# A retention block feeding a two-matmul block: writing the first four steps out by hand, scaling the first chunks on VectorE, and moving the transposes

## The chip, the cores and the metric

The kernel runs on one core of a Trainium2 chip. The metric is the device time of one execution in microseconds (us). A profile is one traced execution. Its span (795.6 us for the kernel before) is about 2 us shorter than the execution's time. TensorE does the matmuls; PSUM is the memory in which the kernel has it put its results, in banks of 128 x 512 float32. "Granted clock" is the share of TensorE's full clock that the profile shows; a group of matmuls that runs at about half of it is called cold here, one at full clock warm. "Step" below means one column group of the second block: h = x w_in for 256 tokens and 256 columns, the nonlinearity, and o += g w_out.

## The reference, cut to what matters

```python
# q, k, v: (4, 8, 768, 64) float32; w_in (512, 2048), w_out (2048, 512) float64
for t in range(S):                                   # retention, as a recurrence
    state = gamma * state + k_t outer v_t
    y_t = q_t @ state / sqrt(64)
x = y.transpose(0, 2, 1, 3).reshape(3072, 512)
h = x @ w_in
out = (h - tanh(h)) @ w_out
```

## The kernel before

The recurrence is computed in 24 chunks of 128 tokens. For a chunk, q and v are scaled by powers of gamma (`scale_chunk`), k and q are transposed on TensorE (`turn`) and copied out of PSUM by ScalarE (`turn_copy`), k'v and k q' are formed (`products`, then mask and states on VectorE), and y is accumulated in two halves (`outputs`). Between the halves other matmuls may stand; ScalarE also touches y there (the "seen" copies). The weights come as float64: 32 pieces, each turned into float32 by two ScalarE, four VectorE and two GpSimd instructions (`convert`). Pieces 0 to 3 are columns of w_in, 4 to 7 rows of w_out, and so on. The first h needs pieces 0 and 1, the second 2 and 3, the first o pieces 4 and 5, the second o 6 and 7.

```python
    def scale_chunk(ci):
        ...
            nc.gpsimd.tensor_tensor(t, t, g[...].to_broadcast([P, H, D]), op=ALU.mult)

    def outputs(ci, meanwhile):
        ...
        intra(True)                  # first half of y
        ...                          # the "seen" copies on ScalarE
        meanwhile()                  # a turn or an up stands here
        intra(False)                 # second half
        nc.scalar.copy(out=xT..., in_=y)
        products(ci + 1)             # the next chunk's mask and states

    for ci in range(AHEAD):          # AHEAD = 3: the start
        scale_chunk(ci + 2)
        outputs(ci, lambda: turn(ci + 2, "h"))
        load_chunk(ci + 3)
        turn_copy(ci + 2)
        convert(ci)
        load_weights(ci + 3)
    for s, (n, m2, first, last) in enumerate(steps):     # from here on h (up), shrink, o (downs)
        ...
```

The order is made by hand (`manual_schedule`): each engine gets its instructions in the order of the calls.

Of the kernel before, what the change touches and what calls it, by code (L numbers as in the profile page):

```python
# [11 lines left out]
U32 = mybir.dt.uint32  # L12
# [3 lines left out]
P = 128  # L16
# [15 lines left out]
def kernel(  # L32
# [20 lines left out]
    nc = tc.nc  # L53
    B, H, S, D = q.shape
    NP = H // 2
# [9 lines left out]
    BANK = 512  # L65
# [45 lines left out]
    def weight_ends(i):  # L111


        f, r = divmod(i, 2 * NC)
        if r < NC:
            c, cols = 2 * (r % 2), ds(BANK * f + TH * (r // 2), TH)
            src = w_in[:, cols].rearrange("(c two p) n -> c two p n", two=2, p=D)

            return w1[:, ds(c, 2), cols], [(0, 0, c, 0, src), (1, 0, c, 1, src),
                                           (0, 1, c + 1, 1, src), (1, 1, c + 1, 0, src)]  # L120
        m = NC * f + r - NC
        return w2[:, m], w_out[ts(m, P)]

    def load_weights(i):
        if i >= NW:
            return
        dst, src = weight_ends(i)
        raw = None
        if w_out.dtype != F32:
            raw = stage.tile([P, 2 * BANK], U32, tag="raw", name=f"raw_{i}", bufs=3)  # L130
            raws[i] = raw
        if not isinstance(src, list):
            if raw is None:
                nc.sync.dma_start(out=dst, in_=src)
            else:
                nc.sync.dma_start(out=raw, in_=src.bitcast(U32))
            return
        for half, k, c, which, w in src:
            r = ds(D * half, D)
            if raw is None:  # L140
                nc.sync.dma_start(out=dst[r, k], in_=w[c, which])
            else:
                nc.sync.dma_start(out=raw[r, ts(k, BANK)], in_=w[c, which].bitcast(U32))  # L143

    def convert(i):

# [37 lines left out]
    def load_chunk(ci):  # L184
        if ci >= NCH:
            return
        b, j = divmod(ci, CPB)
        loaded[ci] = []
        for nm, src in (("k", k), ("q", q), ("v", v)):
            t = inp.tile([P, H, D], F32, tag=nm, name=f"{nm}_{ci}")  # L190
            nc.sync.dma_start(out=t, in_=src[b, :, ts(j, P), :].rearrange("h p d -> p h d"))  # L191
            loaded[ci].append(t)

    def scale_chunk(ci):
        if ci >= NCH:
            return
        j = ci % CPB
        _, qh, vh = loaded[ci]
        for t, g in ((qh, gq), (vh, gv)):
            nc.gpsimd.tensor_tensor(  # L200
                t, t, g[:, ts(j, H)][:, :, None].to_broadcast([P, H, D]), op=ALU.mult
            )

# [27 lines left out]
    def products(ci):  # L231

        if ci >= NCH:
            return
        kh, _, vh = loaded[ci]
        kT, qT = (turned[ci][:, i] for i in range(2))
        sp = banks(f"s_{ci}")
        halves = sp.rearrange("p r (w n t) -> p r w n t", w=2, n=NP)
        for p in range(NP):
            for a in range(2):  # L240
                for i in range(2):
                    h, r = 2 * p + i, ds(D * a, D)
                    nc.tensor.matmul(halves[ds(D * i, D), a, 1, p], kh[r, h], vh[r, h],  # L243
                                     start=True, stop=True, skip_group_check=True)
        for p in range(NP):
            for a in range(2):
                for i in range(2):
                    r = ds(D * i, D)
                    nc.tensor.matmul(halves[ds(D * a, D), i, 0, p], kT[r, p, ts(a, D)],  # L249
                                     qT[r, p, ts(a, D)], start=True, stop=True,  # L250
                                     skip_group_check=True)
        m = mid.tile([P, 2, NP, D], F32, tag="a", name=f"a_{ci}")
        nc.vector.tensor_tensor(m, halves[:, :, 0],  # L253
                                causal[:, None, None, :].to_broadcast([P, 2, NP, D]),
                                op=ALU.mult)
        masked[ci] = m
        j = ci % CPB
        if j == 0:
            states[ci] = mid.tile([P, 2, NP, D], F32, tag="state", name=f"state_{ci}", bufs=3)
            nc.vector.tensor_copy(states[ci][:, 1], halves[:, 0, 1])  # L260
        else:
            nc.vector.tensor_tensor(states[ci][:, 1], halves[:, 0, 1], states[ci][:, 0],
                                    op=ALU.add)
        if j < CPB - 1:
            nxt = mid.tile([P, 2, NP, D], F32, tag="state", name=f"state_{ci + 1}", bufs=3)
            nc.vector.tensor_tensor(nxt[:, 0], halves[:, 1, 1], states[ci][:, 1], op=ALU.add)
            states[ci + 1] = nxt

    def outputs(ci, meanwhile):


        j = ci % CPB
        n, nj = divmod(ci, BLK)
        if nj == 0:
            xT[n] = xp.tile([P, NP, BLK * P], F32, tag="xT", name=f"xT_{n}")
        vh = loaded.pop(ci)[2]
        qT = turned.pop(ci)[:, 1]
        a_, st = masked.pop(ci), states.pop(ci)
        yT = banks(f"y_{ci}")
        y = yT[:, :, : 2 * P].rearrange("p r (n t) -> p r n t", n=2)  # L280
        begun = set()

        def to_y(p, i, a, lhsT, rhs):

            col = (i + p) % 2
            start = (p % 2, col) not in begun
            begun.add((p % 2, col))
            nc.tensor.matmul(y[ds(D * col, D), p % 2, p // 2, ts(a, D)], lhsT, rhs,  # L288
                             start=start, stop=True, skip_group_check=True)

        def inter(a):
            for p in range(NP):
                for i in range(2):
                    r = ds(D * i, D)
                    to_y(p, i, a, st[r, a, p], qT[r, p, ts(a, D)])

        def intra(first):
            for pp in range(NP // 2):
                for i in range(2):
                    for a in range(2):  # L300

                        for col in range(2):
                            p = 2 * pp + ((a + col) % 2 if first else (a + col + 1) % 2)
                            if (i + p) % 2 != col:
                                continue
                            r = ds(D * a, D)
                            to_y(p, i, a, vh[r, 2 * p + i], a_[r, i, p])

        if j:
            inter(0)  # L310
        inter(1)
        intra(True)


        flat = yT.rearrange("p r w -> p (r w)")
        for col in range(2):
            r = ds(D * col, D)
            s0, s1 = 2 * P - 1 - D, BANK + 2 * P - 1
            if col:
                s0, s1 = 2 * P - 1, BANK + 2 * P - 1 - D  # L320
            nc.scalar.copy(out=seen[r], in_=flat[r, s0 : s1 + 1 : s1 - s0])
        meanwhile()
        intra(False)
        nc.scalar.copy(  # L324
            out=xT[n][:, :, ts(nj, P)].rearrange("p (n r) t -> p r n t", r=2), in_=y
        )
        products(ci + 1)


    gT = {}  # L330
# [72 lines left out]
    runs += [[(n, m2) for m2 in range(NM // 2)] for n in range(4, 2 * NB)]  # L403
    steps = [(n, m2, i == 0, i == len(r) - 1) for r in runs for i, (n, m2) in enumerate(r)]



    AHEAD = 3
    when = [0, 1, 2, 3, 4] + list(range(5, 28, 2)) + [28, 29, 30, 31]
    with_chunk = {s: AHEAD + i for i, s in enumerate(when)}  # L410
    with_weights = {0: [3, 4], 1: [5, 6], 2: [7]}
    for i in range(8, NW):
        with_weights[i - 5] = [i]

    load_chunk(0)
    load_chunk(1)
    load_weights(0)
    load_weights(1)
    load_chunk(2)
    load_weights(2)  # L420
    scale_chunk(0)
    turn(0)
    turn_copy(0)
    scale_chunk(1)
    products(0)
    turn(1)
    turn_copy(1)
    for ci in range(AHEAD):
        scale_chunk(ci + 2)
        outputs(ci, lambda: turn(ci + 2, "h"))  # L430
        load_chunk(ci + 3)
        turn_copy(ci + 2)
        convert(ci)
        load_weights(ci + 3)
    waiting = []

    def downs(lag):
# [2 lines left out]
            for j in range(2):  # L440
                down(n, m2, j, first, last)

    for s, (n, m2, first, last) in enumerate(steps):
        for i in with_weights.get(s, []):
            convert(i)
            load_weights(i + 3)
        ci = with_chunk.get(s)
        if ci is None:
            up(n, m2)
        else:  # L450
            scale_chunk(ci + 2)
            outputs(ci, lambda: up(n, m2))
            load_chunk(ci + 3)
        shrink(n, m2)
        waiting.append((n, m2, first, last))
        downs(LAG)
        if ci is not None:
            turn(ci + 2)
            turn_copy(ci + 2)
# [57 lines left out]
```

## Time and profile before

| | before |
|---|---|
| median of the runs | 798.71 us at first (3), 798.47 with one run more |
| span of the profiled run | 795.6 us |
| TensorE busy | 760.5 us, 96% |
| TensorE idle up to 90 us, from stretches of 5 us | 31.0 us |
| lost to the lower clock up to 90 us (busy time x (1 - granted clock), the same stretches) | 13.9 us |

The last two rows are the whole room, the 4.7 us of the first load included: after 80.5 us TensorE is full at full clock until the tail. The lines that show it stand in the prediction.

### The profile page before, as it was taken

The numbers are of one execution on the slowest core, as the hardware profiler recorded it, in microseconds if no ns is written. First come the engines' busy times: TensorE is split into PE (matmuls) and PEld (weight loads), VectorE is DVE, ScalarE is ACT, GpSimd is POOL, SyncE is SP. The second block draws the span as 40 slices with busy tenths as digits, with TensorE's granted clock in tenths as the row PEclk, the third lists the DMA queues.
The fourth block names the chain that finished last, engine by engine and source line by source line (L and its number), as shares of the span: only waits on it lengthen the run. The fifth ranks groups of instructions, "written<-read, shape, count | busy, mean of one in ns | idle before, by whom it ended". The sixth has DMA issues, their size and how long they took to land.

```text
span 795.6 us, 13784 instructions
## 1 busy us (share of the span) xinstructions
PE 760.5 (96%) x5504; PEld 515.9 (65%) x5504; DVE 508.4 (64%) x798; ACT 368.2 (46%) x660; POOL 131.0 (16%) x116
## 2 busy tenths in 40 slices
PE   4558999999999999999999999999999999999997
PEld 3446776666676677666666666666666666666663
DVE  0377777778888876566565666565565666655654
ACT  1344666556565644444444444444444444444442
POOL 2355344335433451000000000000000000000000
PEclk8577999999999999999999999999999999999999
DMA  9555564335444413000000000000000000000000
GB/s 201 140 135 130 121 134 110 105 94 132 111 105 99 116 41 81 29 27 27 1 26 1 0 27 0 1 26 1 1 27 1 15 12 0 28 0 1 27 0 26
DMA packets 85967, 42.97 MB, mean 54 GB/s; under 512 B 76560, under 2 KB 76688, under 8 KB 85904
## 3 DMA queue, kind: packets, MB, share of 16 engines
q1 hardware_dynamic: 85760, 41.95, 21.2%
q8 instruction: 43, 0.70, 0.4%
q10 hardware_dynamic: 144, 0.15, 0.1%
q14 instruction: 20, 0.16, 0.1%
HBM read 35.80 MB, written 6.29 MB: 53 GB/s over the span
## 4 chain that ended last, share of the span: by engine, by line
PE 91%; DVE 3%; POOL 2%; SPq 1%; issue 1%; DMA 1%; ACT 1%; DVEq 0%; POOLq 0%; ACTq 0%
PE h L342 41%; PE o L374 41%; PE y L288 3%; PE kqTp L215 3%; PE s L249 1%; PE s L243 1%; POOL low L171 1%; SPq L191 1%; SPq L143 1%; DMA q<-in_q_dram 1%; POOL w L175 1%; POOL q L200 1%; DVE head L168 1%; DVE head L166 0%; DVE power L170 0%
## 5 line engine op out<-in xcount | busy, mean ns | idle before, releaser
L342 PE MATMUL h<-xT,w 128*128 128x256 f32 x1536 | 351.9, 382 | 0.0
L374 PE MATMUL o<-w,g 128*128 128x512 f32 x768 | 347.2, 595 | 0.5 <-DVE g L366 0.5
L342 PEld LDWEIGHTS h<-xT,w 128*128 128x128 f32 x1536 | 291.1, 191 | 67.5 <-issue 30.4
L374 PEld LDWEIGHTS o<-w,g 128*128 128x128 f32 x768 | 144.2, 190 | 144.8 <-issue 136.8
L351 ACT ACTIVATE u<-h 128x512 f32<-128x512 f32 x96 | 57.4, 598 | 265.0 <-PE h L342 265.0
L356 DVE TENSOR_TENSOR th<-h,th 128x512 f32<-128x512 f32 x96 | 66.2, 690 | 158.2 <-ACT th L352 158.2
L366 DVE COPY_PREDICATED g<-large,th 128x512 f32<-128x512 int32 x96 | 71.6, 745 | 9.9
L359 DVE SCALAR_TENSOR_TENSOR h<-q,h 128x512 f32<-128x512 f32 x96 | 66.9, 696 | 10.0
L361 DVE SCALAR_TENSOR_TENSOR h<-q,h 128x512 f32<-128x512 f32 x96 | 66.8, 696 | 10.0
L353 ACT ACTIVATE q<-u,tab 128x512 f32<-128x512 f32 x96 | 69.5, 724 | 0.0
L354 ACT ACTIVATE q<-u,tab 128x512 f32<-128x512 f32 x96 | 69.1, 720 | 0.0
L355 ACT ACTIVATE large<-u,tab 128x512 f32<-128x512 f32 x96 | 68.8, 717 | 0.0
L365 DVE TENSOR_TENSOR g<-h,u 128x512 f32<-128x512 f32 x96 | 66.3, 691 | 3.3
L253 DVE TENSOR_TENSOR a<-s,tab 128x512 f32<-128x512 f32 x24 | 16.6, 692 | 77.5 <-PE s L249 77.5
L171 POOL TENSOR_TENSOR low<-low,power 128x512 f32<-128x512 f32 x32 | 40.9, 1279 | 152.9 <-DVE power L170 151.7
L357 DVE SCALAR_TENSOR_TENSOR h<-u,h 128x512 f32<-128x512 f32 x96 | 65.8, 685 | 0.0
L352 ACT ACTIVATE th<-h 128x512 f32<-128x512 f32 x96 | 57.1, 595 | 0.0
L324 ACT COPY xT<-y 128x512 f32<-128x512 f32 x24 | 14.1, 586 | 92.7 <-PE y L288 92.7
L225 ACT COPY kqT<-kqTp 128x1024 f32<-128x1024 f32 (+1 forms) x27 | 24.5, 920 | 41.6 <-PE kqTp L215 41.6
L175 POOL TENSOR_TENSOR w<-low,head 128x512 f32<-128x512 f32 x32 | 41.0, 1282 | 2.5
L215 PE MATMUL kqTp<-tab,q 128*128 128x128 f32 x96 | 17.3, 310 | 17.0 <-POOL q L200 17.0
L200 POOL TENSOR_TENSOR q<-q,tab 128x512 f32<-128x512 f32 x24 | 25.5, 1063 | 21.9 <-DMA q<-in_q_dram 21.9
(30 smaller groups left out, 374.2 us busy)
## 6 DMA issues: line engine op xcount, KB each, us to landing
raw<-in_moe_w_in_dram SPq DMA_DIRECT2D x64, 128.0 KB, 2.9
raw<-in_moe_w_out_dram SPq DMA_DIRECT2D x16, 512.0 KB, 3.7
k<-in_k_dram SPq DMA_DIRECT2D x24, 256.0 KB, 4.4
q<-in_q_dram SPq DMA_DIRECT2D x24, 256.0 KB, 5.0
v<-in_v_dram SPq DMA_DIRECT2D x24, 256.0 KB, 4.9
out_dram<-sum SPq DMA_DIRECT2D x24, 256.0 KB, 2.0
tab<-in_tables_dram ACTq DMA_DIRECT2D x1, 145.5 KB, 2.7
```

The source lines that it names most:

```text
L342: nc.tensor.matmul(hp[:, ts(i, TH)], w1[:, c, ts(2 * m2 + i, P)], xT[n // 2][:, c, ts(n % 2, TH)], start=(i == 0 and c == 0), stop=(c == N ...
L351: nc.scalar.activation(u, hp, AF.Square)
L353: nc.scalar.activation(q0, u, AF.Square, bias=bias0)
L354: nc.scalar.activation(q1, u, AF.Square, bias=bias1, scale=math.sqrt(A))
L355: nc.scalar.activation(large, u, AF.Relu, bias=bias_m)
L356: nc.vector.tensor_tensor(th, hp, th, op=ALU.subtract)
L357: nc.vector.scalar_tensor_tensor(hp, in0=u, scalar=R, in1=hp, op0=ALU.subtract, op1=ALU.mult, reverse0=True)
L359: nc.vector.scalar_tensor_tensor(hp, in0=q0, scalar=C0, in1=hp, op0=ALU.add, op1=ALU.mult)
L361: nc.vector.scalar_tensor_tensor(hp, in0=q1, scalar=A * C1, in1=hp, op0=ALU.add, op1=ALU.mult)
L365: nc.vector.tensor_tensor(flat, hp, u, op=ALU.mult)
L366: nc.vector.copy_predicated(flat, large.bitcast(I32), th)
L374: nc.tensor.matmul(o_p[j], gT[n, m2][:, i, ts(j, P)], w2[:, 2 * m2 + i], start=(first and i == 0), stop=(last and i == 1))
```

## The change

The intent: the first h should not wait for four chunks. The start is written out so that each step follows the loads; chunks 0 to 3 are scaled on VectorE; no transposes stand between the halves of another chunk's outputs; and a w_in piece is loaded with three issues instead of four. Piece 2 is now also loaded behind chunk 3 and not ahead of it.

```diff
-            src = w_in[:, cols].rearrange("(c two p) n -> c two p n", two=2, p=D)
-            return w1[:, ds(c, 2), cols], [(0, 0, c, 0, src), (1, 0, c, 1, src),
-                                           (0, 1, c + 1, 1, src), (1, 1, c + 1, 0, src)]
+            return w1[:, ds(c, 2), cols], [
+                (ds(0, P), 0, w_in[ts(c, P), cols]),
+                (ds(0, D), 1, w_in[ds((c + 1) * P + D, D), cols]),
+                (ds(D, D), 1, w_in[ds((c + 1) * P, D), cols]),
+            ]
...
-    def scale_chunk(ci):
+    def scale_chunk(ci, engine=nc.gpsimd):
...
-        meanwhile()
-        intra(False)
-        nc.scalar.copy(...)
-        products(ci + 1)
+        def rest():
+            intra(False)
+            nc.scalar.copy(...)
+        halfway[ci] = rest
...
+    scale_chunk(0, nc.vector); turn(0, "o"); turn_copy(0); scale_chunk(1, nc.vector)
+    products(0); turn(1, "h"); turn_copy(1); outputs(0); products(1); outputs_rest(0)
+    load_chunk(3); load_weights(2); convert(0); load_weights(3)
+    outputs(1); convert(1); load_weights(4); outputs_rest(1)
+    scale_chunk(2, nc.vector); turn(2, "o"); turn_copy(2)
+    up_step(0)
+    products(2); scale_chunk(3, nc.vector); turn(3, "o"); turn_copy(3)
+    convert(2); load_weights(5); outputs(2); products(3); outputs_rest(2)
+    load_chunk(4); convert(3); outputs(3); load_chunk(5); load_weights(6); outputs_rest(3)
+    shrink_step(0)
+    up_step(1); convert(4); load_weights(7); shrink_step(1); scale_chunk(4)
+    convert(5); load_weights(8); up_step(2); turn(4); turn_copy(4); shrink_step(2)
+    downs(LAG)
+    products(4); scale_chunk(5); convert(6); ... convert(7); ... up_step(3); outputs(4) ...
```

(The calls stand one to a line in the source; the tail up to chunk 7 is cut. From the fifth step on there is a loop much as before; in it the conversions now stand behind the first half of the outputs.)

More of the change, by code (lines that the diff above doesn't have):

```diff
@@ L137, in load_weights @@
             return
-        for half, k, c, which, w in src:
-            r = ds(D * half, D)
+        for r, k, w in src:
             if raw is None:
-                nc.sync.dma_start(out=dst[r, k], in_=w[c, which])
+                nc.sync.dma_start(out=dst[r, k], in_=w)
             else:
-                nc.sync.dma_start(out=raw[r, ts(k, BANK)], in_=w[c, which].bitcast(U32))
+                nc.sync.dma_start(out=raw[r, ts(k, BANK)], in_=w.bitcast(U32))
     def convert(i):
@@ L199, in scale_chunk @@
         for t, g in ((qh, gq), (vh, gv)):
-            nc.gpsimd.tensor_tensor(
+            engine.tensor_tensor(
                 t, t, g[:, ts(j, H)][:, :, None].to_broadcast([P, H, D]), op=ALU.mult
@@ L267, in products, with outputs @@
             states[ci + 1] = nxt
-    def outputs(ci, meanwhile):
+    halfway = {}
+    def outputs(ci):
         j = ci % CPB
@@ L289, in to_y @@
                              start=start, stop=True, skip_group_check=True)
-        def inter(a):
-            for p in range(NP):
-                for i in range(2):
-                    r = ds(D * i, D)
-                    to_y(p, i, a, st[r, a, p], qT[r, p, ts(a, D)])
         def intra(first):
@@ L307, in intra @@
                             to_y(p, i, a, vh[r, 2 * p + i], a_[r, i, p])
-        if j:
-            inter(0)
-        inter(1)
+        for a in range(2):
+            if j or a:
+                for p in range(NP):
+                    for i in range(2):
+                        r = ds(D * i, D)
+                        to_y(p, i, a, st[r, a, p], qT[r, p, ts(a, D)])
         intra(True)
@@ L321, in outputs, with outputs_rest @@
             nc.scalar.copy(out=seen[r], in_=flat[r, s0 : s1 + 1 : s1 - s0])
-        meanwhile()
-        intra(False)
-        nc.scalar.copy(
-            out=xT[n][:, :, ts(nj, P)].rearrange("p (n r) t -> p r n t", r=2), in_=y
-        )
-        products(ci + 1)
+        def rest():
+            intra(False)
+            nc.scalar.copy(
+                out=xT[n][:, :, ts(nj, P)].rearrange("p (n r) t -> p r n t", r=2), in_=y
+            )
+        halfway[ci] = rest
+    def outputs_rest(ci):
+        halfway.pop(ci)()
     gT = {}
@@ L404 @@
     steps = [(n, m2, i == 0, i == len(r) - 1) for r in runs for i, (n, m2) in enumerate(r)]
-    AHEAD = 3
-    when = [0, 1, 2, 3, 4] + list(range(5, 28, 2)) + [28, 29, 30, 31]
-    with_chunk = {s: AHEAD + i for i, s in enumerate(when)}
-    with_weights = {0: [3, 4], 1: [5, 6], 2: [7]}
-    for i in range(8, NW):
-        with_weights[i - 5] = [i]
-    load_chunk(0)
-    load_chunk(1)
-    load_weights(0)
-    load_weights(1)
-    load_chunk(2)
-    load_weights(2)
-    scale_chunk(0)
-    turn(0)
-    turn_copy(0)
-    scale_chunk(1)
-    products(0)
-    turn(1)
-    turn_copy(1)
-    for ci in range(AHEAD):
-        scale_chunk(ci + 2)
-        outputs(ci, lambda: turn(ci + 2, "h"))
-        load_chunk(ci + 3)
-        turn_copy(ci + 2)
-        convert(ci)
-        load_weights(ci + 3)
     waiting = []
@@ L441, in downs, with up_step, shrink_step @@
                 down(n, m2, j, first, last)
-    for s, (n, m2, first, last) in enumerate(steps):
+    def up_step(s):
+        n, m2, first, last = steps[s]
+        up(n, m2)
+        waiting.append((n, m2, first, last))
+    def shrink_step(s):
+        shrink(*steps[s][:2])
+    load_chunk(0)
+    load_chunk(1)
+    load_weights(0)
+    load_weights(1)
+    load_chunk(2)
+    scale_chunk(0, nc.vector)
+    turn(0, "o")
+    turn_copy(0)
+    scale_chunk(1, nc.vector)
+    products(0)
+    turn(1, "h")
+    turn_copy(1)
+    outputs(0)
+    products(1)
+    outputs_rest(0)
+    load_chunk(3)
+    load_weights(2)
+    convert(0)
+    load_weights(3)
+    outputs(1)
+    convert(1)
+    load_weights(4)
+    outputs_rest(1)
+    scale_chunk(2, nc.vector)
+    turn(2, "o")
+    turn_copy(2)
+    up_step(0)
+    products(2)
+    scale_chunk(3, nc.vector)
+    turn(3, "o")
+    turn_copy(3)
+    convert(2)
+    load_weights(5)
+    outputs(2)
+    products(3)
+    outputs_rest(2)
+    load_chunk(4)
+    convert(3)
+    outputs(3)
+    load_chunk(5)
+    load_weights(6)
+    outputs_rest(3)
+    shrink_step(0)
+    up_step(1)
+    convert(4)
+    load_weights(7)
+    shrink_step(1)
+    scale_chunk(4)
+    convert(5)
+    load_weights(8)
+    up_step(2)
+    turn(4)
+    turn_copy(4)
+    shrink_step(2)
+    downs(LAG)
+    products(4)
+    scale_chunk(5)
+    convert(6)
+    load_chunk(6)
+    load_weights(9)
+    turn(5)
+    turn_copy(5)
+    convert(7)
+    load_weights(10)
+    up_step(3)
+    outputs(4)
+    products(5)
+    outputs_rest(4)
+    load_chunk(7)
+    shrink_step(3)
+    outputs(5)
+    scale_chunk(6)
+    downs(LAG)
+    outputs_rest(5)
+    load_chunk(8)
+    turn(6)
+    turn_copy(6)
+    products(6)
+    scale_chunk(7)
+    turn(7)
+    turn_copy(7)
+    BEGUN = 4
+    when = [4, 5, 6] + list(range(7, 28, 2)) + [28, 29, 30, 31]
+    with_chunk = {s: 6 + i for i, s in enumerate(when)}
+    with_weights = {4: [8], 5: [9, 10]}
+    for i in range(11, NW):
+        with_weights[i - 5] = [i]
+    for s in range(BEGUN, len(steps)):
+        ci = with_chunk.get(s)
+        if ci is not None:
+            scale_chunk(ci + 2)
+            outputs(ci)
         for i in with_weights.get(s, []):
@@ L446 @@
             load_weights(i + 3)
-        ci = with_chunk.get(s)
-        if ci is None:
-            up(n, m2)
-        else:
-            scale_chunk(ci + 2)
-            outputs(ci, lambda: up(n, m2))
+        up_step(s)
+        if ci is not None:
+            outputs_rest(ci)
+            products(ci + 1)
             load_chunk(ci + 3)
-        shrink(n, m2)
-        waiting.append((n, m2, first, last))
+        shrink_step(s)
         downs(LAG)
```

## The prediction

> **What bounds the kernel now.** I read the slices of the page first, then the table of stretches, then the timeline of each engine in the stretch that is not full. TensorE is 96% busy over the span of 795.6 us, and the slices say where it is not:
>
> ```profile
> PE   4558999999999999999999999999999999999997
> ...
> PEclk8577999999999999999999999999999999999999
> ```
>
> Each digit is a slice of 19.9 us. Only the first four are poor, both in busy share and in granted clock. The stretches give this its size:
>
> ```profile
> core 0: us, PE busy (x) PEld busy (x) DVE busy (x) ACT busy (x) POOL busy (x), PEclk, DMA share, GB/s
> 0.00:80.50 80.50, 49.54 (x921) 40.50 (x921) 37.15 (x61) 28.20 (x56) 35.68 (x35) 0.72 0.66 152
> 80.50:340.00 259.50, 259.50 (x3029) 179.37 (x3026) 196.41 (x335) 146.31 (x272) 95.37 (x82) 1.00 0.41 97
> 340.00:795.60 455.60, 451.43 (x1560) 296.06 (x1560) 274.82 (x402) 193.65 (x334) 0.00 (x0) 1.00 0.03 12
> ```
>
> After 80.5 us TensorE never idles and has its full clock until a tail of 4.2 us (455.60 - 451.43). Nothing reordered there can gain. Up to 80.5 us it idles 31.0 us, and weighting its busy time by the clock of 5 and 10 us stretches gives another 13.8 us lost to a lower clock. So some 45 us are lost, of which 4.7 (the first load) can't be saved: at most about 40 us, 5%, is at stake. Who is waited for in there:
>
> ```profile
> PE kqTp L215 <- POOL q L200: 17.0, 6, 4.1
> PE kqTp L215 <- DMA k<-in_k_dram: 9.0, 2, 4.7
> PE y L288 <- ACT seen L321: 2.5, 1, 2.5
> PE y L288 <- DVE state L262: 2.2, 3, 0.7
> ```
>
> The transposes of q wait for GpSimd's scaling, and being between the halves of another chunk's outputs they hold that chunk's masks, state and copy back too. GpSimd for its part waits for weight conversion on VectorE, which stands behind that chunk's mask: a loop of about 11 us per chunk (q transposed at 19.32, 30.13, 41.00). The first matmul of the real work:
>
> ```profile
> 45.90 0.41 PE L288 MATMUL y<-a,v 64*64 64x64 f32 x16
> 46.24 3.72 PE L342 MATMUL h<-xT,w 128*128 128x256 f32 x16
> 52.51 0.71 PE L288 MATMUL y<-a,v 64*64 64x64 f32 x16 [2.55 <-ACT seen L321]
> ```
>
> The groups of h follow at 46.24, 62.34 and 74.78, and the first group of o at 80.48.
>
> [...] four 128x128 transposes take 1.11 us at 25.00 and 0.60 at 84.02, and h takes 5.53 us at 62.34 after a pause. It also shows idle times of only 2.6 and 2.7 us (before 52.51 and 72.53) being followed by slow matmuls. [...]
>
> ```profile
> 49.86 1.64 DVE L168 SCALAR_TENSOR_TENSOR head<-raw,head 128x512 uint32<-128x512 uint32 x1
> 51.60 0.43 DVE L170 TENSOR_SCALAR power<-head 128x512 uint32<-128x512 uint32 x1
> ```
>
> That L168 takes 0.69 us when GpSimd is idle, and ends 0.55 us after GpSimd's add of 49.62 to 50.95. [...] the trace has 0.69 for L365. So scaling moved to VectorE costs 0.69 us instead of GpSimd's 1.04, but may have to wait for GpSimd.
>
> **The change part by part.**
> (a) w_in loads: 3 issues for 4 per piece. In before a piece's further issues take 0.59 us on the queue plus 0.04; two pieces stand ahead of chunk 2, so that chunk is issued some 1.3 us sooner (11.0 for 12.29). The bytes are the same and the queue was near full in 5 to 15 us, so I count 1 us at most, and this lies in a time in which the new order has other work.
> (b) Chunks 0 to 3 scaled on VectorE: 8 instructions of 0.69 (5.5 us of VectorE[...]) for 8 of 1.04 on GpSimd. Against it: [...] the scale of v_1 (landed at 10.96) now stands before the mask of chunk 0. The mask slips from 10.43 to about 11.65, the first output from 12.06 to 12.7.
> (c) Order. The same matmuls, 5504. I walk the new order of each engine with before's durations: VectorE conversion 2.0 us alone, 3.9 beside GpSimd; GpSimd 2.6 per conversion; shrink 2.8 on ScalarE and 4.4 on VectorE, starting 1.0 after h; mask and states 1.5; the "seen" copies 0.35; group h 3.65 at full clock, o 3.6, products 1.05, outputs 1.1, turn 1.0.
>
> Chunks 0 and 1 run through without a chunk 2: outputs of chunk 1 are over at 17.0 (31 in before). Conversion of w piece 0 runs on VectorE 15.8 to 17.8 and GpSimd to 20.5; piece 1 on VectorE to 21.5 [...], and piece 1 is ready at 25.3. TensorE has nothing between 18 and 22 but k_2, so the first h starts at 25.3 (46.24 in before) at half clock and takes about 6.2 us: 31.5. Products of 2 end at 32.5, its mask and states at 34.0, the scales of chunk 3 at 35.3, its transposes at 35.2; conversion 2 follows to 38.3, the mask of chunk 3 to 39.7, conversion 3 to 42.5. Outputs of 2 and 3 are over at 40.9. Piece 3 leaves GpSimd at 45.2, and the second h (columns of pieces 2 and 3) starts there, cold again: to 50.9. The third h is free to follow: 54.6. The shrink of the second h holds VectorE until 56.4, and only after it comes conversion 5: 58.4, GpSimd to 61.0. The first o needs that piece of w_out and stands ahead of all else on TensorE, idle from 55.6. It runs 61.0 to 67.1 (cold). Then without a wait products 4 (68), turn 5, the fourth h (72.7), outputs 4, products 5. Conversions 6 and 7 stand behind the mask of chunk 4: 69.6, 71.6, 75.1, GpSimd to 77.8. The second o therefore starts at 77.8 and ends at 81.4.
>
> Sum. At 81.4 the new order has done, against what before had done at 80.5: one h more (3.65) and two o more (7.2), one turn and one products less (1.0 + 1.05), that is 8.8 us of full-clock work. It is 0.9 us later: 7.9 us gained. Off this I take 1 us for what comes next: the copy of xT and the sums stand in a row on ScalarE before the copy of chunk 6, and chunk 7 is only issued after w pieces 9 and 10, at about 76.6, and lands at about 82. After that, both kernels are bound by the same 706 us of TensorE work. The gain is 7 us: 798.7 - 7 = 791.7, and I say 791.5.
>
> **Rivals.**
> 1. The reorder takes most of the stall away. For it: h starts 21 us sooner, VectorE is busy only 37.15 of the first 80.5 us and GpSimd 35.68, so neither is full. It would bring a fill of about 65 us in place of 80, 783 or less. Against: VectorE, GpSimd and TensorE take turns in one chain here (mask, conversion, multiply and add, matmul), and the low busy shares are the sign of a chain, not of room.
> 2. A wait for weights takes the place of the wait for q. The o groups wait for pieces 5 and 7 in my walk, and piece 7 comes at 77.8 against 79.9 in before. I hold this for right. If each conversion on VectorE meets GpSimd, it is another 2 us for each of four: no gain, 797 to 799.
> 3. The early loads were the bound (chunk 2 is waited for up to 5.2 us in the chain of waits), and fewer issues give the gain alone: about 1 us, 797.5. Against: after 20 us the loads are only waited for through buffers that conversions free.
> 4. The clock decides. Three times (h at 25.3 and 45.2, o at 61.0) the new order starts cold[...]
>
> **Range and chances.** The middle is 791.5. Two conversions or masks worse than walked, or a stall I don't see around chunks 6 and 7, make it 796; [...] shorter stalls at the two o groups 785. I take 784.5 to 796.5. Faster by over 2% needs under 782.7, 16 us gained out of at most 40: rival 1, 0.09. Slower by over 2% needs a new stall of 16 us: 0.01. Within 2%: 0.90.
>
> **What would show it.** In the changed kernel: the first h near 25 us (right if 23 to 28) and the second near 45 after a wait for GpSimd's last conversion step; the first o near 61 and the second near 78, both waiting for w_out pieces from GpSimd; the wait of transposes for GpSimd's q nearly gone; TensorE idle up to 81 us still 25 us or more and the clock there still well below 1; VectorE's scales of 0.7 us, one of chunk 2's up to 2 us. TensorE full from about 84 us. It is wrong if the o groups start without a wait, before 60 and 70 us (then 783 or less), or if TensorE has idle times after 90 us (then 796 or more).

What the trace of before shows: VectorE's L168 took 1.64 us beside GpSimd and 0.69 while GpSimd was idle (49.86 and 46.85), L166 1.38 and 0.43 (48.44 and 46.39); after 2.55 us of idle TensorE's granted clock was 0.50 in 52.5 to 54.0 us, after 2.74 us it was 0.58 in 72.5 to 74.8.

The sum came to 798.7 - 7 = 791.7, given as 791.5. Piece 1 at 25.3 us lies 3.8 us behind the 21.5 of VectorE, of which GpSimd's conversion is 2.6. The lengths of the cold groups (6.2 us for the first h, 5.7 for the second, 6.1 for the first o) are my estimates; the second h of before took 5.53.

## The result, and the profile after

The changed kernel took 791.18 us (790.02 to 791.66, 4 runs) against 798.47 us, ratio 0.9908 with a 95% interval of 0.9891 to 0.9925. Ratios here are the mean time of one kernel's runs over the mean of the other's runs of the same rounds, so they are not quite the ratio of the medians. Executions over 1.5% slower than the fastest of the same kernel are left out of the means. Run again unaltered on another chip, it gave 792.88 us and 0.9928 (0.9915 to 0.994). So some 5.5 to 7.3 us are gained, and between calls some 2 us are not to be told apart.

The slices of the page, after:

```profile
PE   4769999999999999999999999999999999999997
...
PEclk9777999999999999999999999999999999999999
```

Slices two and three are fuller, but the digits still fall short of 9. The stretches (columns as in the prediction):

```profile
0.00:80.50 80.50, 55.91 (x868) 39.95 (x872) 48.67 (x81) 33.55 (x65) 27.89 (x26) 0.81 0.66 154
80.50:340.00 259.50, 258.20 (x3102) 179.70 (x3103) 202.80 (x330) 146.71 (x268) 98.61 (x82) 1.00 0.40 97
340.00:789.40 449.40, 445.18 (x1540) 292.04 (x1538) 270.62 (x396) 190.25 (x328) 0.00 (x0) 1.00 0.03 12
```

Up to 80.5 us TensorE is 6.4 us busier (55.91 for 49.54), at 0.81 of its clock for 0.72, and the tail is the same 4.2 us. In stretches of 5 us up to 90 us, idle time went from 31.0 to 25.7 us and the loss to the clock from 13.9 to 11.4: 7.6 us together, of which the span shows 6.2. What TensorE waits for (total us, times, longest):

```profile
PE o L378 <- POOL w L176: 5.3, 1, 5.3
PE kqTp L216 <- DMA k<-in_k_dram: 4.5, 1, 4.5
PE kqTp L216 <- DVE q L201: 4.3, 3, 1.7
PE y L290 <- issue: 3.5, 2, 2.8
```

The 17.0 us of waits for GpSimd's q are gone. In their place is one wait of the first o for GpSimd's conversion, waits for VectorE's scales, and a wait for nothing ("issue"). TensorE's timeline (start, duration, instruction, and in brackets the idle time before it and what ended that), cut to the marks of the prediction:

```profile
18.22 0.26 PE L290 MATMUL y<-kqT,state 64*64 64x64 f32 x1 [2.79 <-issue]
...
23.91 5.51 PE L346 MATMUL h<-xT,w 128*128 128x256 f32 x16
...
40.30 2.07 PE L346 MATMUL h<-xT,w 128*128 128x256 f32 x4
44.08 8.17 PE L346 MATMUL h<-xT,w 128*128 128x256 f32 x28 [1.70 <-POOL w L176]
...
52.95 1.02 PE L378 MATMUL o<-w,g 128*128 128x512 f32 x2
59.24 5.49 PE L378 MATMUL o<-w,g 128*128 128x512 f32 x6 [5.27 <-POOL w L176]
...
75.10 5.40 PE L378 MATMUL o<-w,g 128*128 128x512 f32 x8
```

The first h starts 22.3 us sooner than the 46.24 of before and is cold: 5.51 us for the 3.65 that such a group takes at full clock. The second h does its first four matmuls with piece 2 at 40.30; its other twelve and the third h's sixteen stand in one row at 44.08, behind GpSimd's last instruction on piece 3. The first o does two matmuls with piece 4, then waits 5.27 us for piece 5. (The profile shows two matmuls for each call of these groups.) The row at 18.22, a pause of 2.79 us that the profile puts down to nothing waited for, is a mark that the prediction does not have.

A check on the size: the fifth h starts at 86.03 us, at 95.95 before. By then the new order has done one chunk less, 3.1 us of work (turn 0.97, products 1.05, outputs 1.1 at full clock): 9.9 - 3.1 = 6.8 us ahead, near the 6.2 us of the spans.

### The profile page after: what moved, and what is told of

The parts are those of the page before. It is cut to its first block, busy times and chain, and to the rows that moved or that the text cites. A ratio compares the mean times of both kernels' runs of the same rounds, so it can differ in the third digit from the quotient of the medians.

```text
span 789.4 us, 13758 instructions
## 1 busy us (share of the span) xinstructions
PE 759.3 (96%) x5504; PEld 511.7 (65%) x5504; DVE 522.1 (66%) x806; ACT 370.5 (47%) x661; POOL 126.5 (16%) x108
## 4 chain that ended last, share of the span: by engine, by line
PE 90%; DVE 6%; issue 1%; POOL 1%; DMA 1%; ACT 1%; SPq 1%; DVEq 0%; ACTq 0%; POOLq 0%
PE h L346 42%; PE o L378 41%; PE y L290 3%; PE kqTp L216 2%; PE s L250 1%; PE s L244 1%; DVE head L169 1%; DVE head L167 1%; DVE a L254 1%; DMA v<-in_v_dram 1%; SPq L192 1%; DVE power L171 0%; DVE g L370 0%; DVE head L165 0%; DVE state L267 0%
## 5 line engine op out<-in xcount | busy, mean ns | idle before, releaser
L378 PE MATMUL o<-w,g 128*128 128x512 f32 x768 | 351.8, 601 | 5.8 <-POOL w L176 5.3
L370 DVE COPY_PREDICATED g<-large,th 128x512 f32<-128x512 int32 x96 | 74.6, 777 | 9.9
L169 DVE SCALAR_TENSOR_TENSOR head<-raw,head 128x512 uint32<-128x512 uint32 x32 | 25.5, 797 | 1.1
L201 POOL TENSOR_TENSOR q<-q,tab 128x512 f32<-128x512 f32 x20 | 21.8, 1089 | 22.2 <-DMA q<-in_q_dram 22.2
```

What stands on the lines that cost most here:

```text
L370: nc.vector.copy_predicated(flat, large.bitcast(I32), th)
L378: nc.tensor.matmul(o_p[j], gT[n, m2][:, i, ts(j, P)], w2[:, 2 * m2 + i], start=(first and i == 0), stop=(last and i == 1))
```

## The experiments

Twelve kernels were run, each in five rounds beside the kernel before; all gave correct results. One of them, after_again, is the changed kernel unaltered. The first four shared a chip and its runs of before (797.79 us), the next four another (797.95), then three (798.36), then one (798.29).

### The loads alone (b_loads)

The three-issue form of `weight_ends` and `load_weights` put into the kernel before, nothing else.

> The kernel before with part (a) alone: w_in pieces in three issues instead of four, everything else as it was. If fewer issues give the gain (rival 3 of the prediction), this takes most of the 7 us: about 792. My theory: the loads are only the first link; chunk 2 is issued some 1.3 us sooner and lands some 1 us sooner, and since the kernel before waits for exactly that (k of chunk 2, then q), its first slices shift by up to 1 us: 797.5 to 798.5 us, ratio 0.9985 to 1.000.

Measured: 797.86 us, ratio 1.0001 (0.9987 to 1.0014). The profile shows the shift and its loss: the first h starts at 45.20 (46.24 before) and the third at 73.99 (74.78), but the third then takes 5.50 us in place of 4.45, because more of it ran at half clock (granted 0.50 up to 77 us; before, up to 76), and the first o starts at 80.75 for 80.48. The loads give no measurable time.

### VectorE's scaling alone (b_dve)

```diff
-            nc.gpsimd.tensor_tensor(
+            (nc.vector if ci < 4 else nc.gpsimd).tensor_tensor(
```

> The kernel before with the scaling of chunks 0 to 3 on VectorE and its order otherwise unchanged (the scales of chunk 3 then stand on VectorE before chunk 2's mask instead of behind a weight conversion on GpSimd). From the timeline of before: q of chunk 3 is ready at about 26.6 instead of 30.1 us, so one of the loops of 11 us becomes one of 7.5, and the rest follows 3 to 3.6 us sooner: 795 us, ratio 0.9955 (0.994 to 0.997). If the engine that scales is what the gain comes from, it is 792. If the order decides all, it is 798.5.

Measured: 794.5 us, ratio 0.9955 (0.9943 to 0.9968), as expected. TensorE's timeline of this kernel:

```profile
19.38 1.11 PE L215 MATMUL kqTp<-tab,q 128*128 128x128 f32 x4 [0.69 <-DVE q L200]
...
27.13 1.09 PE L215 MATMUL kqTp<-tab,q 128*128 128x128 f32 x4 [0.96 <-DVE q L200]
...
37.98 1.11 PE L215 MATMUL kqTp<-tab,q 128*128 128x128 f32 x4 [4.08 <-POOL q L200]
```

From chunk 2 to chunk 3 it is 7.75 us, and from 3 to 4, where GpSimd scales again, 10.85 us. One loop was shortened by 3 us and that is what the time shows.

### The order with GpSimd's scaling (a_pool)

The changed kernel with `scale_chunk(0)` to `scale_chunk(3)` in place of `scale_chunk(0, nc.vector)` and so on.

> The changed kernel with the scaling of chunks 0 to 3 back on GpSimd, order unchanged. Theory (order decides, the engine of the scaling little): chunk 0's mask is about 1 us sooner, the first h starts 3 us later (about 27) since q of chunk 2 waits behind two conversions on GpSimd, but q of chunk 3 is ready without a wait, which gives back 1.7 us; in all 1 to 1.5 us slower than the changed kernel, 792.4, ratio to before 0.992 to 0.9935. If scaling on VectorE is half of the gain or more, it is 795 or slower.

Measured: 790.96 us, ratio 0.9912 (0.9899 to 0.9926): not told apart from the changed kernel. The marks are where they were expected:

```profile
26.39 1.12 PE L216 MATMUL kqTp<-tab,q 128*128 128x128 f32 x4 [6.69 <-POOL q L201]
27.30 5.10 PE L346 MATMUL h<-xT,w 128*128 128x256 f32 x16
...
33.92 0.60 PE L216 MATMUL kqTp<-tab,q 128*128 128x128 f32 x4
```

The first h is 3.4 us later, and chunk 3's q is transposed without a wait. The loss of 1 to 1.5 us that I expected does not show: the second h's first matmuls stand at 40.85, where the changed kernel's two profiles have 40.30 and 41.34, so the delay was gone by then. Together with b_dve this is a two by two table: old order 1 and 0.9955 (GpSimd, VectorE), new order 0.9912 and 0.9908 (or 0.9928 in the control). The engine of the scaling matters in the old order, where the scale stands behind a conversion on GpSimd. In the new order it doesn't show. So the gain comes from the order. Which part of the order gives it is not separated further, except for the place of the transposes (next run); and the new order was not run with the old loads.

### Transposes back between the halves (a_between)

```diff
-    outputs_rest(1)
     scale_chunk(2, nc.vector); turn(2, "o"); turn_copy(2)
+    outputs_rest(1)
...
-    turn(3, "o"); turn_copy(3)
     convert(2); load_weights(5)
     outputs(2)
-    products(3)
+    turn(3, "o"); turn_copy(3)
     outputs_rest(2)
+    products(3)
```

> The changed kernel with the transposes of chunks 2 and 3 put back between the halves of the outputs of chunks 1 and 2 (their scaling and copies moved with them). Theory: chunk 1's second half then waits for q of chunk 2 until about 24 us, its xT copy is done at about 25.3 and the first h starts 1.5 us later than 23.9; for chunk 3 the same costs about 1 us more. So 1 to 2.5 us slower than the changed kernel: 792 to 793.7, ratio to before 0.992 to 0.994. If those transposes were the main cost of the old order, it is 795 or slower.

Measured: 790.35 us, ratio 0.9906 (0.9892 to 0.9919). This is a miss: no loss. The first part came as expected, the rest did not:

```profile
25.89 6.24 PE L346 MATMUL h<-xT,w 128*128 128x256 f32 x16 [0.80 <-ACT xT L324]
...
45.25 7.71 PE L346 MATMUL h<-xT,w 128*128 128x256 f32 x28 [2.57 <-POOL w L176]
...
75.65 4.05 PE L378 MATMUL o<-w,g 128*128 128x512 f32 x8
```

The first h is 2.0 us later, the second 1.2 (44.08 in the first profile of the changed kernel, 45.60 in the control's), the second o 0.55, and that o then takes 4.05 us instead of 5.40, since it got the full clock sooner. The first h is later than in both profiles of the changed kernel (23.91 and 24.89); from the second h on, the delay is within what those two differ by, and in this one the second o ran at full clock (granted 1.00, where it was 0.52 in 75.1 to 77.0 us of the changed kernel). Whatever the transposes cost between the halves here, it is under what these runs can show.

### Conversion 5 sooner (a_conv5)

```diff
     up_step(1); convert(4); load_weights(7)
-    shrink_step(1); scale_chunk(4)
     convert(5); load_weights(8)
+    shrink_step(1); scale_chunk(4)
```

> The changed kernel with conversion 5 (the w_out piece that the first o waits for from 53.6 to 59.2 us) moved ahead of the second shrink. Theory: it is on the chain, and VectorE's position of it decides: VectorE is done with it at about 52.4 beside GpSimd instead of 56.4, GpSimd at about 56 instead of 59.2, the first o follows 3 us sooner, and since nothing else then binds, the kernel is 2 to 3.5 us faster than the changed one: 788.2, ratio to before 0.987 (0.986 to 0.9885). Rival: the chain through the second shrink and chunk 4's mask takes over and less than 1 us is gained.

Measured: 788.31 us, ratio 0.9882 (0.9869 to 0.9895), as expected.

```profile
57.40 1.12 PE L216 MATMUL kqTp<-tab,q 128*128 128x128 f32 x4 [2.58 <-POOL q L201]
58.31 4.78 PE L378 MATMUL o<-w,g 128*128 128x512 f32 x8
```

The first o runs from 58.31 us without a wait and is done at 63.02 (64.66 in the changed kernel's profile), although this profile's start was the later one: its second h stood at 45.80. The wait for piece 5 is on the path, and VectorE's order sets it. Part of it came back at once: chunk 4's q, now scaled behind conversion 5 on GpSimd, is waited for 2.58 us ahead of the o.

### Conversions 4 and 5 sooner (a_conv45)

```diff
-    shrink_step(0); up_step(1)
     convert(4); load_weights(7)
-    shrink_step(1); scale_chunk(4)
     convert(5); load_weights(8)
+    shrink_step(0); up_step(1)
+    shrink_step(1); scale_chunk(4)
```

> The changed kernel with conversions 4 and 5 both ahead of the first shrink. Theory: GpSimd has piece 5 at about 51.7, the first shrink ends at about 53.4 on VectorE, the third h waits for its bank until about 52.7, and the first o runs from about 56.4 to 60 (64.7 in the changed kernel): 4 to 5 us faster than the changed kernel, 786.7, ratio to before 0.985 (0.984 to 0.987). If the later shrinks become the bound, no faster than the other move alone.

Measured: 791.43 us, ratio 0.9922 (0.991 to 0.9934). A miss: nothing gained over the changed kernel, and 3 us behind a_conv5 on the same chip.

```profile
54.28 6.46 PE L346 MATMUL h<-xT,w 128*128 128x256 f32 x16 [3.82 <-ACT q L358]
```

The third h takes the PSUM bank of the first and so waits for the first shrink, whose last instruction that reads the bank ran from 53.45 to 54.14 us on VectorE (the profile names a ScalarE instruction that ended at 54.17, but that one reads no PSUM bank). I had put that at 52.7, and had the third h warm. After 3.82 us of idle it was cold: 6.46 for 3.65 us. Those two, 1.6 and 2.8 us, are most of the 5.1 us by which the first o was late (61.46 for 56.4). Ahead of the second o, chunk 5's state was then waited for 2.66 us, where the changed kernel waited 0.86.

### Fillers that keep TensorE busy (a_warm)

```diff
+    first = bank("o", "warm_first")
+    for _ in range(10):
+        nc.tensor.transpose(first[:, :P], ident, ident)
     turn(2, "o")
...
+    warm(10)          # the same, into a spare bank
     up_step(1)
...
+    warm(34)
     downs(LAG)
```

> The changed kernel with 10, 10 and 34 transposes of the identity into a spare bank, put in front of chunk 2's transposes, of the second h and of the first o, where TensorE waits anyway (results unchanged). They only keep it busy. Theory: the groups of h at 23.9 and 44.1 and of o at 59.2 then run at full clock, 3.65 and 3.6 us instead of 5.5, and as all three are on the chain, 3 to 5 us are gained: 787.5, ratio to before 0.9865 (0.985 to 0.9885). Rival: the clock doesn't matter there because the next wait (for VectorE) ends when it did, or the fillers only take time: 791 or more.

Measured: 786.79 us, ratio 0.9862 (0.9848 to 0.9877): 54 useless transposes make the kernel some 4 to 5 us faster.

```profile
24.28 4.60 PE L346 MATMUL h<-xT,w 128*128 128x256 f32 x16
...
43.50 6.31 PE L346 MATMUL h<-xT,w 128*128 128x256 f32 x28 [0.78 <-POOL w L176]
...
57.35 2.84 PE L378 MATMUL o<-w,g 128*128 128x512 f32 x6 [1.19 <-POOL w L176]
```

The same groups took 5.51, 8.17 and 5.49 us in the changed kernel. The rest of the first o takes about half the time, and it starts 1.9 us sooner. VectorE's timeline says why: the second h was over sooner, so the second shrink began at 47.51 instead of 49.94, conversion 5 behind it at 52.40 instead of 54.29, and GpSimd was done with piece 5 at 57.30 instead of 59.18. During the 34 fillers the granted clock was 1.00. So the clock is on the path, not only beside it.

### Chunk 3 loaded later (a_late3)

```diff
-    load_chunk(3)
...
     outputs_rest(1)
+    load_chunk(3, nc.scalar)
```

> The changed kernel with chunk 3's loads issued from ScalarE's queue after it has copied chunk 1's xT, so at about 21 us instead of 14 to 18. In the changed kernel TensorE stops for 2.79 us at 15.4 in the middle of chunk 1's outputs, where no semaphore is waited for; an instruction-fetch packet is moved in that stretch, in which the data queue fills all 16 DMA engines. If the fetch waits behind the data, the pause shrinks to about 1 us, conversion 1 starts sooner and the kernel is about 1 us faster than the changed one (790). If the pause has another cause, it stays at 2.8 us and the time at 791 to 791.5.

Measured: 792.67 us, ratio 0.9927 (0.9915 to 0.9939), and the pause was 3.01 us. The expectation of a shorter pause fell. It is not a clean test of my guess that a fetch stood behind the data: the loads of chunk 2 and piece 2 still kept the DMA engines full until 18 us (their packets took 105 to 126% of the 16 engines' time in each us from 14 to 18). In all kernels of the new order the pause comes at the same instruction, after 30 of the first 32 matmuls of chunk 1's y, lasts 1.5 to 3.4 us in the profiles and ends between 17.7 and 19.2 us, and a packet of the instruction queue moves between 14 and 17 us (15.54 to 16.85 in the changed kernel). The packed traces hold the packet's own times: it lands between 16.3 and 17.7 us, and in all eleven profiles TensorE goes on 1.4 to 1.7 us after that, whether the pause was short or long. So the end of the pause goes with the packet. In the old order, where such a packet moves too (14.16 to 15.11 in before), TensorE comes to these matmuls at about 22.6 us, long after it. No run moved the packet: that TensorE waits for it is not shown, nor why it comes late.

### Control, and three steps further (after_again, c1, c2, c3)

> The changed kernel unaltered, as a control beside the next two on the same chip: 791 us, ratio to before 0.9908 (0.989 to 0.9925) as at first.

Measured: 792.88 us, 0.9928.

c1 is a_warm (24 fillers for 34) with conversion 5 ahead of the second shrink and chunk 4's scale ahead of conversion 5.

> Conversion 5 ahead of the second shrink and the fillers together (24 instead of 34 ahead of the first o), with chunk 4's scaling ahead of conversion 5 on GpSimd, since with the move alone chunk 4's q waited 2.6 us behind that conversion. Each alone took 3 to 4.5 us off the changed kernel. If wait and clock are separate costs, the gains add for the most part: the first o starts without a wait near 55 us and runs in 3.6 us, 784.5 us, ratio 0.983 (0.981 to 0.985). If the fillers already take what the move takes (both shorten the same chain to the first o), it is no better than the fillers alone: 786.5 to 787.5.

Measured: 786.66 us, ratio 0.9858 (0.9844 to 0.9873). The first o came as expected, and the gain did not:

```profile
54.85 3.60 PE L378 MATMUL o<-w,g 128*128 128x512 f32 x8
...
69.79 0.70 PE L290 MATMUL y<-kqT,state 64*64 64x64 f32 x16 [2.55 <-DVE state L263]
```

The first o starts 0.3 us sooner than in a_warm (54.85 for 55.14), has no wait in it and is over 1.7 us sooner (58.38 for 60.12). But chunk 5's mask on VectorE stands behind the third shrink and conversions 6 and 7, and this link now waits 2.55 us, where a_warm waited 0.85. The second o starts at 70.85 for 70.46.

c2 adds to c1: chunk 3 scaled on GpSimd, `convert(1)` ahead of `outputs(1)`, and 4 fillers for 10 at the first place.

> The same, and the two waits left ahead of the second h cut: chunk 3 scaled on GpSimd, which is idle then (the transposes of chunk 3 waited 1.7 us for VectorE), and conversion 1 on ScalarE ahead of chunk 1's seen copies, so that TensorE's pause in the middle of those outputs no longer holds VectorE (2.8 us idle at 17.4); 4 fillers instead of 10 at the first place. If both waits are on the chain, the second h's wait for piece 3 ends 2 to 3 us sooner than in c1: 782, ratio 0.980 (0.978 to 0.982). If [...] the loads take their place, it is within 0.5 us of c1.

Measured: 784.75 us, ratio 0.984 (0.9823 to 0.9856), 1.9 us better than c1 by the medians, though the intervals overlap, and 2.8 us short of the 782 expected.

```profile
38.77 8.71 PE L346 MATMUL h<-xT,w 128*128 128x256 f32 x32
...
52.43 3.60 PE L378 MATMUL o<-w,g 128*128 128x512 f32 x8
...
67.98 5.60 PE L378 MATMUL o<-w,g 128*128 128x512 f32 x8
```

The second h's wait for piece 3 was gone and the first o stood at 52.43 (54.85), as expected; the second o, 2.9 us sooner than in c1, started cold and took 5.60 us instead of 4.73.

c3 puts `convert(6)` where the third shrink stood, the third shrink behind the rest of chunk 4's outputs, and the fourth behind the products of chunk 6.

> c2 with the third and fourth shrinks put behind the masks they held up, and conversion 6 in the time in which VectorE waited for them. In c1 and c2 the wait moved on: chunk 5's outputs waited 2.55 us for its mask, which stood on VectorE behind the third shrink and conversions 6 and 7, and the second o then started cold (5.6 us for 3.6). If that is the next link, chunk 5's outputs start at about 64.5 instead of 67.4 us without a wait and the second o takes 3.6 to 4 us: 4 to 5 us faster than c2, 780, ratio to before 0.978 (0.976 to 0.9805). If the shrinks put off come back as a wait of TensorE or ScalarE later (for a bank, or for the copies of chunk 6), less than 2 us are gained.

Measured: 784.09 us, ratio 0.982 (0.9804 to 0.9837), the lowest median, but short of the 780 expected and, on another chip, not told apart from c2. The named link did go:

```profile
68.80 0.69 PE L290 MATMUL y<-kqT,state 64*64 64x64 f32 x32 [0.72 <-ACT xT L324]
...
69.66 3.70 PE L378 MATMUL o<-w,g 128*128 128x512 f32 x8
```

Chunk 5's outputs no longer wait for VectorE, and the second o is warm. From the first o to the fifth h it is 24.28 us (26.69 in c2), so 2.4 us were gained there, not 4 to 5: chunk 5's q now waited 2.04 us for GpSimd, behind conversion 6. And this profile lost about as much ahead of the first o (54.61 for 52.43): its first h ran cold (6.24 us), and piece 3 was waited for again (2.45 us).

## Why the prediction was right

The time (791.5 predicted, 791.18 measured), the direction and the size came out, and so did the mechanism up to the first o. At the second o the wait was another one than predicted, and inside the walk errors of both signs nearly cancelled, which is in part luck. By steps:

**Only the start is at stake.** After 92 us the new kernel's TensorE idles 0.15 us up to 340 us, then has the same tail. Right.

**(a) Loads, "1 us at most".** Measured 0 (b_loads).

**(b) Scaling.** VectorE's scales take 0.69 us as said, and one of chunk 2's 1.76 us beside GpSimd, where up to 2 was said. The slip of chunk 0's mask was oversized: it ran at 11.00 us and not 11.65, because v of chunk 1 landed by 10.39 and not 10.96.

**(c) The walk.** First h 25.3 predicted, 23.91 and 24.89 in the two profiles; second h 45.2, and 44.08 and 45.60; third h over at 54.6, and 52.1 and 53.9; first o free to run at 61.0, and 59.24 and 61.07; second o 77.8, and 75.10 and 77.05. The pause of 2.79 us in chunk 1's outputs was not in the walk: these were over at 20.2 us, 17.0 predicted, and conversion 1 on VectorE began at 20.20. But by then GpSimd was done with piece 0 (20.14 us), so conversion 1 took 2.1 us in place of the 3.7 that I had put for it beside GpSimd (17.8 to 21.5), and ended at 22.34 for 21.5. A second slip stands in four places: I had each group wait as a whole for the later of its two pieces, but the first part needs only the earlier one. The first h began at 23.91, before GpSimd was done with piece 1 (25.74, 25.3 predicted); the second h did four matmuls at 40.30; the first o did two with piece 4, 1.0 us of work in time that was idle anyway; and the second o began with piece 6.

**The wait at the second o.** I had it wait for piece 7 from GpSimd. It began at 75.10 without a wait of its own, right behind chunk 5's outputs, which had waited 0.72 us for ScalarE's copy and 0.86 us for VectorE's state; a weight load inside it waited 0.75 us for piece 7, which GpSimd finished at 76.26. The two pauses, with 1.11 us of work in the 2.7 us from 72.4 to 75.1, were followed by a granted clock of 0.52 up to 77.0 us, and this o took 5.40 us instead of 3.7. The link there is chunk 5's mask and state, behind conversions 6 and 7 on VectorE, as c1 and c3 confirm.

**The sum.** The second o was over at 80.4 us, 81.4 predicted, and the two small waits behind it, put at 1 us, were 0.48 and 0.67 us; the first is for ScalarE's copy of chunk 6, as I had said, the second for VectorE's states and not for the load of chunk 7. The 706 us of TensorE work that both kernels are said to share stand in no view (the stretches of before give 710.9 after 80.5 us); nothing rests on that number. The gain of 7 us was 7.3 in the first runs and 5.5 in the control.

**The rivals.** Rival 2 (weights take the place of q) is shown at the first o: GpSimd's w is the longest wait now, and a_conv5 took 2 to 4 us off (against the two measurements of the changed kernel) by moving that conversion. Rival 3 (loads) fell with b_loads. Rival 4 (the clock) was right that the new order starts cold, and more than once: the cold starts cost 1.9 us at the first h, 1.8 at the second and third, 2.8 at the first o and 1.7 at the second (time taken less the time of as many matmuls at full clock). The fillers, with which the three groups of a_warm's timeline above took 4.60, 6.31 and 2.84 us for 5.51, 8.17 and 5.49, gave 4 to 5 us. Rival 1 (most of the stall goes) did not happen, for the reason given against it: each of a_conv5, c1 and c3 took one link away and the next one took over part or all.

Of the signs listed, four were off. The second o did not wait for GpSimd. TensorE's idle time up to 80.5 us was 24.6 us (80.50 - 55.91) where "25 us or more" was said; the first two matmuls of the first o ran at 52.95, before 60 us, though the wait was where it was predicted; and TensorE was full from 85.4, not 84 us.

What my expectations got wrong afterwards: that transposes between the halves cost 1 to 2.5 us (a_between, none seen), that scaling on GpSimd costs 1 to 1.5 us in the new order (a_pool, none seen), that moving conversions ahead of shrinks is free (a_conv45: the shrinks free the PSUM banks, and the third h waited 3.82 us for its bank), and that gains found one by one add up (c1, c2 and c3 each came 2 to 4 us short of the middle expected).

## What to carry to other kernels

When several engines hand work to each other in a ring and none of them is full, walk the new order by hand with durations from the old trace; here that placed five marks within 3 us and the total within 1.4, with errors of both signs. Look for work that needs only the first of two operands: it starts before the walk says so (the first h at 23.91 us, its second piece done at 25.74). Moving a step to a faster engine (a scale takes 0.69 us on VectorE, 1.04 on GpSimd) paid where it stood behind other work (3.3 us in the old order) and not where the delay was gone again before it reached the next link (none seen in the new). Before shortening a wait, ask what stands on the same engine behind it and what clock TensorE will have when it ends (the second o of c2 stood 2.9 us sooner than in c1 and took 5.60 us instead of 4.73): a few dozen useless transposes in the waits were worth at least as much as the best single move (786.79 and 788.31 us on the same chip).
